# SSM kernel generation with 64-row TensorE tiles: phases and coarse decays as two products side by side

## The chip, the cores and the metric

The kernel runs on one core of a Trainium2 chip. A core has TensorE (matrix products, PE in the profile; its weight loads are PEld), VectorE (DVE), ScalarE (ACT), GpSimd (POOL) and SyncE (SP), which issues the DMA transfers; SBUF is its working memory and PSUM takes the products. Every engine works through its own instruction stream in order and waits on semaphores for the others. The metric is the device time of one execution in microseconds (us); lower is better.

## The reference, cut to what matters

Two branches are mixed by a gate. Branch A is a diagonal state-space layer: for each of D = 640 channels a kernel K of length L = 2048 is generated from N = 128 complex modes, and convolved with the input by FFT. Branch B is a feed-forward layer of width 1728 with a ReLU.

```
dt = exp(log_dt)
A = -exp(log_A_real) + 1j * A_imag
C = (C_real + 1j * C_imag) * dt[:, None]
P = exp((A * dt[:, None])[:, :, None] * pos[None, None, :])
K = 2.0 * einsum("dn,dnl->dl", C, P).real
...
y = irfft(rfft(u_t, 2L) * rfft(K, 2L), 2L)[:, :, :L]
a = y.T + u * D_skip
b = relu(x @ w1) @ w2
g = sigmoid((u * gate_w).sum(-1))
out = g * a + (1 - g) * b
```

## The kernel before

The work is added as tasks to a planner (class `Plan`). Each task has an engine, a queue, a booked duration, the tasks it depends on and the buffers it takes and frees. `run` (line 160) goes through the queues, picks the next task for each engine by priority and readiness, and emits its instructions; so the booked durations decide the order of the instructions on every engine, and the order is fixed when the kernel is built. On TensorE each task also has a mode, and a change of mode is booked at 0.2 us (line 108). All engine calls go through one helper, which is why all profile lines carry L228; operations are told apart by the names of their tiles.

The feed-forward branch (`feed_forward`, line 278) runs in 3 parts of 5, 5 and 4 blocks of 128 hidden units, each over 8 groups of 256 positions. Values are split in a high and a low float32r part (`xh`, `xl`, `w1h`, `w1l`, `hh`, `hl`, `w2h`, `w2l`), and three products stand for one float32 product. `hidden` (line 396) computes ReLU(x w1) with products of 256 columns, `sums` (line 442) the second layer with products of 320 columns; both write PSUM tiles `pf`. ScalarE takes the high part (`hh`), VectorE the low part (`hl`), and VectorE adds the sums into `q`. Weight tiles are split into `w1l` and `w2l` by VectorE. From the second part on, x is loaded again from DRAM (`xh`, `xl` from `xt`), and partial sums go out to `part` and come back as `q`.

The SSM kernel K is generated in 40 blocks of C = 16 channels (`ssm`, line 742). For each block c one tile R[c] of 128 rows (16 channels times 8 values: high and low parts of the angle per step, an offset angle, and the decay rate) by 128 modes is the stationary operand. It is multiplied with a constant table `tg` that has 128 rows and a block per channel:

- phases (line 792): `pg` = 16 channels x 64 positions, two products of 512 columns, table columns 0 to 1023;
- coarse decays (in `exponents`, line 815): `px` = 16 x 64, two products of 512 columns, table columns 1024 to 2047;
- fine decays (line 826): `pe` = 16 x 32, one product of 512 columns, table columns 2048 to 2559.

Row 8d + k of R belongs to channel d of the block, and the table is zero except where row and column belong to the same channel. So the first product of `pg` has entries only in rows 0 to 63, the second only in rows 64 to 127; the same holds for `px`.

The three are joined on TensorE to one visit (line 925). After a visit ScalarE rounds the phase (`cs`<-`pg`), VectorE takes the remainder (`sn`) and its absolute value (`cs`), ScalarE computes exponentials (`me`, `mg`) and sine and cosine, and VectorE multiplies them (`factors`, line 851: `G`, `mg`, `cs`, `sn`). Every second block `taps` (line 880) forms the kernel values in 128x32 tiles of TensorE (`pk`), VectorE turns them (`kt`), GpSimd adds the skip term and SP stores them to `kd`.

The convolution (`conv`, line 936) starts when all of `kd` is stored. It runs 5 rounds of 128 channels with small FFT matrices as 64x64 and 128x64 tiles of TensorE (`pc`): first stage for the kernel (`ck`) and the input (`ut`) with the table `tf`, second stage (`vk,tm` and `va,tm`), a product on VectorE (`t`), an inverse second stage (`t,tn`), turns on VectorE (`vk`, `va`) and an inverse first stage (`vk,tw`). Feed-forward products stand between its instructions where the planner found room.

Before all this, `params` (line 612) computes rates and angles from the inputs, and loads the table `t_g` in pieces of 512 columns, which ScalarE casts to float32r into `tg` (lines 719 to 728).

Of the kernel before, what the change touches and what calls it, by code (L numbers as in the profile page):

```python
# [10 lines left out]
F32 = mybir.dt.float32  # L11
F32R = mybir.dt.float32r
# [9 lines left out]
PARTS = (5, 5, 4)  # L22
CG = (0, 0, 0, 1, 2, 3, 4, 5)
FIRST = 7
BEHIND = 3

# [1 line left out]
def slots():  # L30
    return np.concatenate([np.arange(32, 64), np.arange(31, -1, -1)])
# [5 lines left out]
def tables():  # L37
    a = np.arange(64)
    k1 = 2 * np.arange(32)[None, :] + np.arange(2)[:, None]
    al = 2 * np.pi * (k1[..., None] + 0.25) * a / 64  # L40
    f1 = np.stack([np.cos(al), np.sin(al)]).transpose(3, 1, 0, 2).reshape(64, 128)
    w = np.stack([np.cos(al), np.sin(al)], axis=1) / 2048
    b = np.arange(32)
    om = 2 * np.pi * (k1[:, :, None, None] + 0.25 + 64 * b[None, None, :, None]) * b / 2048
    c, s = np.cos(om), np.sin(om)
    m = np.zeros((2, 2, 32, 32, 3, 32))
    n = np.zeros((2, 2, 32, 32, 2, 2, 32))
    iw = np.zeros_like(w)
    for p in range(2):
        ct, st = c[p].transpose(2, 0, 1), s[p].transpose(2, 0, 1)  # L50
        m[p, 0, :, :, 0], m[p, 0, :, :, 1] = ct, st
        m[p, 1, :, :, 0], m[p, 1, :, :, 1] = -st, ct
        m[p, :, :, :, 2] = m[p, :, :, :, 0]
        for g in range(32):
            h = p ^ (g & 1)
            ck, sk = c[p, g], s[p, g]
            re, im = np.stack([ck, -sk], axis=1), np.stack([sk, ck], axis=1)
            n[h, 0, :, g, 0], n[h, 1, :, g, 0] = re, -re
            n[h, 0, :, g, 1], n[h, 1, :, g, 1] = im, im
            iw[p, :, g // 2 * 2 + h] = w[p, :, g]  # L60

    pt, mg, me = np.zeros((16, 8, 16, 64)), np.zeros((16, 8, 16, 64)), np.zeros((16, 8, 16, 32))
    for d in range(16):
        pt[d, :2, d, :32], pt[d, :2, d, 32:], pt[d, 2:4, d, :32] = b, 32 * b + 16, 1
        mg[d, 4:6, d], me[d, 4:6, d] = 32 * slots(), b
    tg = np.concatenate([x.reshape(128, -1) for x in (pt, mg, me)], axis=1)
    f = lambda x: np.ascontiguousarray(x.astype(np.float32))
    return dict(t_g=f(tg), t_f1=f(np.tile(np.stack([f1, f1[slots()]], axis=1), (2, 1, 1))), t_w=f(iw.reshape(128, 64)),
                t_m=f(m.reshape(128, 32, 96)), t_n=f(n.reshape(128, 32, 128)))
# [180 lines left out]
class Kernel:  # L250
# [361 lines left out]
    def params(self):  # L612
        tc, nc, io, A = self.tc, self.nc, self.io, self.plan.add
# [65 lines left out]
        R = lambda f: (lambda V: f(V, *T_()))  # L679
# [36 lines left out]
        done = [*last['a'], *last['c'], *self.rows_st[0], *self.rows_st[1]]  # L716
        self.tg_done, tok = [], self.plan.token
        self.plan.ring('tgs', 2)
        for h in range(5):
            s_ = tok('tgs')  # L720

            def load(h=h):
                tl['tgs', h] = tl['pp'].tile([128, 512], F32, name="tgs", bufs=2)
                D_.dma_start(tl['tgs', h], io['t_g'][:, h * 512:h * 512 + 512])
            a = A('SP', 'tg', 0.62, load, [self.prm0], take=[s_], kb=256, rank=6)
            self.late_loads.append(a)
            self.tg_done.append(A('ACT', 'tg', 0.63, lambda h=h: S.copy(self.tg[:, h * 512:h * 512 + 512], tl['tgs', h]),
                                  [a], use=[s_], rank=4))

        p_ = tok('px')  # L730

        def cm_pe():
            px = self.psg.tile([128, 4, 256], F32, name="px")
            tl['pe'] = px.rearrange("p a b -> p (a b)")[:, :D].rearrange("p (t d) -> p t d", d=128)
            for t in range(NT):
                self.E.transpose(tl['pe'][:, t], tl['mx'][:, t], self.ident)
        a = A('PE', 'cm', 1.1, cm_pe, last['c'], take=[p_], rank=2, mode='f')
        self.cm_done = A('ACT', 'cm', 1.2, lambda: S.copy(self.cm[:].rearrange("p (t d) -> p t d", d=128), tl['pe']), [a],
                         use=[p_], rank=1)
        return [*done, *self.tg_done, self.cm_done, a]  # L740

    def ssm(self, C=16):
        tc, nc, io, A, tok, ring = self.tc, self.nc, self.io, self.plan.add, self.plan.token, self.plan.ring
# [5 lines left out]
        self.xp = gk  # L749
        self.c_ps, self.psg = self.cm_enter(name="psg", bufs=1, space=PSUM)  # L750
        self.cm = gk.tile([128, D], F32, name="cm")
        self.tg = gk.tile([128, 2560], F32R, name="tg")
        dsk = gk.tile([128, n // 2, 2 * Q], F32, name="dsk")
        nc.gpsimd.memset(dsk, 0.0)
        for k, v in dict(pg=1, px=1, pk=1, sc=5, mg=4, G=2, kt=2, PS=2).items():
# [10 lines left out]
        st = {}  # L766
# [4 lines left out]
        opened = self.prm_shut = A('PY', 'open', 0, go, self.params())  # L771
        self.prm_open = opened
        R, rows = {}, {}
# [14 lines left out]
        tasks, f = {}, {}  # L788
# [3 lines left out]
        def phases(c):  # L792
            p_, s_ = tok('pg'), tok('sc')
            rd, r_ = rows[c]

            def pe():
                p = self.psg.tile([128, 4, 256], F32, name="pg")
                pf = p.rearrange("p d j -> p (d j)")
                st['pg'] = pf.rearrange("p (d j) -> p d j", j=64)
                for h in range(2):  # L800
                    x = slice(h * 512, h * 512 + 512)
                    self.E.matmul(pf[:, x], R[c], self.tg[:, x], start=True, stop=True)

            def whole():
                st['sc', c] = [st['gp'].tile([128, C, 64], F32, name=k, bufs=5) for k in ("sn", "cs")]
                S.copy(I(st['sc', c][1]), st['pg'])
            a = visit[c, 1] = A('PE', None, 0.5, pe, [rd, opened, *self.tg_done], take=[p_], use=[r_], rank=2, mode='f')
            b = acts[c, 0] = A('ACT', None, 0.97, whole, [a], take=[s_], use=[p_], rank=2)
            d = A('DVE', 'g1', 1.14, lambda: V.tensor_sub(st['sc', c][0], st['pg'], I(st['sc', c][1])), [b],
                  use=[p_, s_], rank=1)  # L810
            e = A('DVE', 'g1', 0.62, lambda: V.tensor_scalar(I(st['sc', c][1]), I(st['sc', c][0]), 0x7fffffff, None,
                                                             op0=ALU.bitwise_and), [d], use=[s_], rank=1, port=True)
            tasks[c] = dict(s=s_, abs=e)

        def exponents(c):
            p_, m_ = tok('px'), tok('mg')
            rd, r_ = rows[c]

            def pe():
                p = self.psg.tile([128, 4, 256], F32, name="px")  # L820
                pf = p.rearrange("p d j -> p (d j)")
                st['px', c] = pf.rearrange("p (d j) -> p d j", j=64)
                for h in range(2):
                    x = slice(h * 512, h * 512 + 512)
                    self.E.matmul(pf[:, x], R[c], self.tg[:, 1024 + h * 512:1536 + h * 512], start=True, stop=True)
                q = st['pe', c] = self.psg.tile([128, C, 32], F32, name="pe")
                self.E.matmul(q.rearrange("p d j -> p (d j)"), R[c], self.tg[:, 2048:], start=True, stop=True)

            def exps(k):
                def go():  # L830
                    if k:
                        st['mg', c] = st['gp'].tile([128, C, 64], F32, name="mg", bufs=4)
                        S.activation(st['mg', c], st.pop(('px', c)), AF.Exp)
                    else:
                        st['me', c] = st['gp'].tile([128, C, 32], F32, name="me", bufs=4)
                        S.activation(st['me', c], st.pop(('pe', c)), AF.Exp)
                return go
            a = visit[c, 2] = A('PE', None, 0.7, pe, [rd, opened, *self.tg_done], take=[p_], use=[r_], rank=2, mode='f')
            b = acts[c, 1] = A('ACT', None, 0.52, exps(0), [a], take=[m_], use=[p_], rank=2, mode='exp')
            d = acts[c, 2] = A('ACT', None, 0.96, exps(1), [b], use=[p_, m_], rank=2, mode='exp')  # L840
            e = A('POOL', 'g2', 1.2, lambda: P.tensor_mul(st['me', c], st['me', c], self.cm[:, c * C:c * C + C, None]
                                                          .to_broadcast([128, C, 32])), [b, self.cm_done], use=[m_])
            s_ = tasks[c]['s']
            h, o = TWO_PI, tasks[c]['abs']
            x = acts[c, 3] = A('ACT', None, 1.0, lambda: S.activation(st['sc', c][0], st['sc', c][0], AF.Sin, scale=h), [o],
                  use=[s_], rank=2, mode='sin')
            y = acts[c, 4] = A('ACT', None, 1.06, lambda: S.activation(st['sc', c][1], st['sc', c][1], AF.Sin, scale=-h,
                                                          bias=self.half_pi), [o], use=[s_], rank=2, mode='sin')
            tasks[c].update(m=m_, exps=[d, e], trig=[x, y])
# [60 lines left out]
        visit, acts = {}, {}  # L910
        for c in range(n):
            if c % 8 == 0:
                load_rows(c)
            phases(c)
            exponents(c)
            factors(c)
# [10 lines left out]
        for p in range(n // 2 + 1):  # L927
            c = 2 * p
# [280 lines left out]
```

## Time and profile before

| | |
|---|---|
| time, median of 3 runs | 719.56 us (719.55 to 720.75) |
| profiled execution | 716.08 us, its span 714.3 us |
| granted TensorE clock, mean | 0.99 |
| visits of the generation on TensorE | 40, from 102.6 to 395 us |
| first product of the convolution | 441.6 us |
| first product of its second stage | 470.6 us |

The rows quoted below are of two kinds. A row of the order of time begins with the start and the length of an instruction or a run of equal ones in us; then come engine, line, operation, output<-inputs, and on TensorE the tile (rows*columns of the array that are used), the shape of the operand that streams and the count. Lengths on TensorE overlap, because products are pipelined and their ends are modelled; what one product costs is read from start to start. A row of busy times by stretch gives the stretch, its length, and for each engine the time that it was busy and the number of its instructions, then the granted clock, the share of the DMA engines' time and the rate.

### The profile page before, as it was taken

How to read it: one execution, taken by the hardware profiler on the slowest of the kernel's cores; microseconds unless marked ns; L12 is line 12 of the kernel's file. 1: busy time of each engine (PE TensorE's matmuls, PEld its weight loads, DVE VectorE, ACT ScalarE, POOL GpSimd, SP SyncE). 2: the span in 40 equal slices, each digit the busy share in tenths (PEclk: the TensorE clock that was granted, in tenths of full speed). 3: DMA queues.
4: the chain of work that ended last, by engine and by line, in shares of the span. 5: the costliest groups of instructions: out<-in, count | busy, mean ns of one | idle time of the engine just before them, and what ended most of it. 6: DMA issues, size and time to landing. Idle time of an engine off the chain costs nothing.

```text
span 714.3 us, 21601 instructions
## 1 busy us (share of the span) xinstructions
PE 672.8 (94%) x9469; PEld 594.5 (83%) x9469; DVE 574.4 (80%) x833; ACT 389.2 (54%) x572; POOL 71.4 (10%) x81
## 2 busy tenths in 40 slices
PE   5989999999999999999999999999699999699897
PEld 4989999889898899999999998887297587487695
DVE  4689628989999999999999873667969879479675
ACT  4353339989888978878888720134151341241330
POOL 1000002111122211122111100000000000010020
PEclk9999999999999999999999999999999999899999
DMA  8963764334556424423422659951643924731534
GB/s 202 260 236 137 272 207 148 86 124 164 164 206 225 146 93 140 160 68 132 160 93 91 235 198 315 290 180 50 140 109 119 225 76 161 139 88 56 121 97 96
DMA packets 92005, 110.83 MB, mean 155 GB/s; under 512 B 30912, under 2 KB 73416, under 8 KB 91656
## 3 DMA queue, kind: packets, MB, share of 16 engines
q1 hardware_dynamic: 91912, 109.46, 51.2%
q8 instruction: 74, 1.21, 0.7%
q14 instruction: 19, 0.16, 0.1%
HBM read 70.24 MB, written 39.20 MB: 153 GB/s over the span
## 4 chain that ended last, share of the span: by engine, by line
PE 69%; DVE 16%; ACT 8%; issue 2%; DMA 2%; SPq 2%; POOLq 0%; DVEq 0%; ACTq 0%
PE pf L228 42%; PE pc L228 18%; PE pk L228 5%; DVE sn L228 3%; ACT cs L228 2%; DVE vk L228 2%; PE pg L228 2%; DVE G L228 2%; DVE mg L228 2%; SPq L228 2%; PE px L228 1%; DVE cs L228 1%; DVE hl L228 1%; ACT L228 1%; ACT sn L228 1%
## 5 line engine op out<-in xcount | busy, mean ns | idle before, releaser
L228 PE MATMUL pf<-xh,w1h 128*128 128x256 f32 x560 | 163.3, 292 | 0.3 <-DVE hl L228 0.3
L228 PE MATMUL pf<-xl,w1h 128*128 128x256 f32 x560 | 160.4, 287 | 0.4 <-DVE xl L228 0.4
L228 PE MATMUL pf<-xh,w1l 128*128 128x256 f32 x560 | 159.9, 285 | 0.0
L228 PE MATMUL pf<-w2h,hh 128*128 128x320 f32 x448 | 140.4, 316 | 3.9 <-DVE hl L228 3.2
L228 PE MATMUL pf<-w2l,hh 128*128 128x320 f32 x448 | 137.9, 311 | 0.0
L228 PE MATMUL pf<-w2h,hl 128*128 128x320 f32 x448 | 126.8, 312 | 0.8 <-DVE hl L228 0.8
L228 PEld LDWEIGHTS pf<-xh,w1h 128*128 128x128 f32 x560 | 109.1, 195 | 6.7 <-issue 4.2
L228 PEld LDWEIGHTS pf<-xl,w1h 128*128 128x128 f32 x560 | 109.2, 195 | 1.6 <-DVE xl L228 0.7
L228 PEld LDWEIGHTS pf<-xh,w1l 128*128 128x128 f32 x560 | 109.3, 195 | 0.0
L228 ACT ACTIVATE hh<-pf 128x512 fp32r<-128x512 f32 (+1 forms) x64 | 34.8, 543 | 127.7 <-PE pf L228 122.0
L228 PEld LDWEIGHTS pf<-w2h,hh 128*128 128x128 f32 x448 | 84.1, 188 | 16.3 <-issue 7.2
L228 PEld LDWEIGHTS pf<-w2l,hh 128*128 128x128 f32 x448 | 84.2, 188 | 5.5 <-issue 4.9
L228 DVE TENSOR_TENSOR t<-pc,kw 128x512 f32<-128x512 f32 x80 | 53.8, 691 | 42.0 <-ACT kw L228 42.0
L228 PEld LDWEIGHTS pf<-w2h,hl 128*128 128x128 f32 x448 | 80.7, 188 | 8.3 <-issue 5.9
L228 POOL TENSOR_TENSOR me<-me,cm 128x512 f32<-128x512 f32 x40 | 50.5, 1262 | 182.3 <-DVE cs L228 103.9
L228 DVE TENSOR_TENSOR mg<-mg,cs 128x1024 f32<-128x1024 f32 x40 | 58.2, 1454 | 1.1
L228 DVE SCALAR_TENSOR_TENSOR hl<-pf,hh 128x512 fp32r<-128x512 f32 (+1 forms) x64 | 39.7, 623 | 20.4 <-ACT hh L228 20.2
L228 ACT COPY kw<-pc 128x256 f32<-128x256 f32 x80 | 29.7, 373 | 47.5 <-PE pc L228 44.9
L228 ACT ACT_TABLE_LOAD x42 | 53.9, 1283 | 0.8
L228 DVE TENSOR_TENSOR sn<-pg,cs 128x1024 f32<-128x1024 f32 x40 | 48.7, 1218 | 6.5 <-ACT cs L228 6.0
L228 PE MATMUL pc<-va,tm 64*64 64x128 f32 x1280 | 53.4, 275 | 0.0
L228 ACT CAST cs<-pg 128x1024 int32<-128x1024 f32 x40 | 40.4, 1010 | 22.0 <-PE pg L228 21.8
(138 smaller groups left out, 1221.5 us busy)
## 6 DMA issues: line engine op xcount, KB each, us to landing
part<-q SPq DMA_DIRECT2D x16, 640.0 KB, 3.8
xh<-xt SPq DMA_DIRECT2D x16, 640.0 KB, 6.6
xl<-xt SPq DMA_DIRECT2D x16, 640.0 KB, 5.2
q<-part SPq DMA_DIRECT2D x16, 640.0 KB, 4.1
ws<-in_B_w_dram SPq DMA_DIRECT2D x22, 320.0 KB, 3.5
xs<-in_A_u_dram SPq DMA_DIRECT2D x16, 320.0 KB, 4.0
xt<-xh SPq DMA_DIRECT2D x8, 640.0 KB
xt<-xl SPq DMA_DIRECT2D x8, 640.0 KB
```

Of the source, the lines that this page charges most:

```text
L228: return lambda *a, **k: self._tc.keep_in_program_order(f(*a, **k))
```

## The change

The table keeps one 8-channel block of 64 rows for phases and one for coarse decays, each 512 columns wide, and holds it twice, in rows 0 to 63 and 64 to 127. The fine decays keep their table. The whole table has 1536 columns instead of 2560, and is loaded and cast in three pieces instead of five. Each of the two products of `pg` and `px` takes 64 rows of R[c] and the same 64 rows of the table, and writes the half of the output that it wrote before, in its own PSUM bank. The product for `pe` is unchanged, with 128 rows. The planner's booked durations for the visit go from 0.5 + 0.7 to 0.3 + 0.55 us; the tasks' mode stays 'f', as for feed-forward products. An unused constant goes.

```diff
-    tg = np.concatenate([x.reshape(128, -1) for x in (pt, mg, me)], axis=1)
+    tg = np.concatenate([np.tile(x[:8, :, :8].reshape(64, -1), (2, 1)) for x in (pt, mg)] + [me.reshape(128, -1)], axis=1)
...
-        for h in range(5):
+        for h in range(3):
             s_ = tok('tgs')
...
-        self.tg = gk.tile([128, 2560], F32R, name="tg")
+        self.tg = gk.tile([128, 1536], F32R, name="tg")
...
                 for h in range(2):
-                    x = slice(h * 512, h * 512 + 512)
-                    self.E.matmul(pf[:, x], R[c], self.tg[:, x], start=True, stop=True)
+                    r = slice(64 * h, 64 * h + 64)
+                    self.E.matmul(pf[:, h * 512:h * 512 + 512], R[c][r], self.tg[r, :512], start=True, stop=True)
...
-            a = visit[c, 1] = A('PE', None, 0.5, pe, [rd, opened, *self.tg_done], take=[p_], use=[r_], rank=2, mode='f')
+            a = visit[c, 1] = A('PE', None, 0.3, pe, [rd, opened, *self.tg_done], take=[p_], use=[r_], rank=2, mode='f')
...
+                q = st['pe', c] = self.psg.tile([128, C, 32], F32, name="pe")
                 for h in range(2):
-                    x = slice(h * 512, h * 512 + 512)
-                    self.E.matmul(pf[:, x], R[c], self.tg[:, 1024 + h * 512:1536 + h * 512], start=True, stop=True)
-                q = st['pe', c] = self.psg.tile([128, C, 32], F32, name="pe")
-                self.E.matmul(q.rearrange("p d j -> p (d j)"), R[c], self.tg[:, 2048:], start=True, stop=True)
+                    r = slice(64 * h, 64 * h + 64)
+                    self.E.matmul(pf[:, h * 512:h * 512 + 512], R[c][r], self.tg[r, 512:1024], start=True, stop=True)
+                self.E.matmul(q.rearrange("p d j -> p (d j)"), R[c], self.tg[:, 1024:], start=True, stop=True)
...
-            a = visit[c, 2] = A('PE', None, 0.7, pe, [rd, opened, *self.tg_done], take=[p_], use=[r_], rank=2, mode='f')
+            a = visit[c, 2] = A('PE', None, 0.55, pe, [rd, opened, *self.tg_done], take=[p_], use=[r_], rank=2, mode='f')
```

More of the change, by code (lines that the diff above doesn't have):

```diff
@@ L24 @@
 FIRST = 7
-BEHIND = 3
 def slots():
```

## The prediction

> **What bounds the kernel now.** I read the page first, then the busy times by stretch. The stretches are cut where the program changes: the first visit of the SSM generation (102.7 us), the last one (395), the first product of the convolution (441.7), its second stage (470.6).
>
> ```profile
> span 714.3 us, 21601 instructions
> ...
> PE 672.8 (94%) x9469; PEld 594.5 (83%) x9469; DVE 574.4 (80%) x833; ACT 389.2 (54%) x572; POOL 71.4 (10%) x81
> ```
>
> ```profile
> core 0: us, PE busy (x) PEld busy (x) DVE busy (x) ACT busy (x) POOL busy (x), PEclk, DMA share, GB/s
> ...
> 102.70:395.00 292.30, 284.14 (x3988) 266.04 (x3987) 273.74 (x378) 253.22 (x299) 57.53 (x57) 1.00 0.41 135
> 395.00:441.70 46.70, 45.89 (x570) 44.49 (x572) 30.92 (x46) 18.99 (x26) 1.78 (x3) 1.00 0.79 242
> 441.70:470.60 28.90, 28.75 (x215) 21.83 (x215) 19.45 (x25) 2.63 (x4) 0.00 (x0) 1.00 0.92 287
> 470.60:520.00 49.40, 43.57 (x886) 31.79 (x889) 38.08 (x51) 18.23 (x43) 0.00 (x0) 1.00 0.47 119
> ```
>
> TensorE is busy 94% of the span, but the reader is to see three kinds of stretch. From 102.7 to 395, TensorE idles 292.3 - 284.1 = 8.2 us and VectorE 18.6 us: both are nearly full and wait on each other. From 395 to 470.6 TensorE alone is full (1.0 us idle in 75.6) and VectorE has a third free. From 470.6 to 520 TensorE has holes of 5.8 us; the chain of waits of that stretch says why:
>
> ```profile
> by line: PE pc L228 45.0%; DVE vk L228 31.4%; DVE va L228 10.6%; issue 3.0%; DVE hl L228 2.2%; PE pf L228 2.1%; DVE t L228 1.4%; ACT yj L228 1.3%; ACT yo L228 1.3%; DVE yj L228 1.3%; ACT kw L228 0.8%
> ```
>
> There the convolution's own chain runs, over VectorE's turns for 42%; feed-forward products (pf) hold 2.1% of it and only fill holes.
>
> **One visit.** Phases (pg), coarse decays (px) and fine decays (pe) of one block stand together on TensorE, 40 times:
>
> ```profile
> 203.01 0.31 PE L228 MATMUL pf<-w2l,hh 128*128 128x320 f32 x1
> 203.16 0.63 PE L228 MATMUL pg<-tg,PS 128*128 128x512 f32 x2
> 203.62 0.64 PE L228 MATMUL px<-tg,PS 128*128 128x512 f32 x2
> 204.09 0.40 PE L228 MATMUL pe<-tg,PS 128*128 128x512 f32 x1
> 204.33 0.30 PE L228 MATMUL pf<-w2h,hl 128*128 128x320 f32 x1
> ```
>
> Start to start, a visit takes 204.33 - 203.16 = 1.17 us: five products of 0.234 us. Starts are used because the durations overlap. A feed-forward product of 320 columns takes 203.16 - 203.01 = 0.15 us (0.147 over a run of them), one of 256 columns 0.12 us (below).
>
> **What the edit does to a visit.** The two products of pg become two of 64 rows each, on the upper and lower half of the array; so do those of px. If the halves run side by side, two of five streams go: -0.47 us. But the array's shape changes twice per visit, 128 rows to 64 and back for pe. The trace has no 64x128 tile, so the price is taken from its nearest rows, the 64x64 tiles of the convolution between feed-forward products:
>
> ```profile
> 493.97 0.28 PE L228 MATMUL pf<-xl,w1h 128*128 128x256 f32 x1
> 494.09 0.28 PE L228 MATMUL pf<-xh,w1l 128*128 128x256 f32 x1
> 494.30 1.09 PE L228 MATMUL pc<-ut,tf 64*64 64x512 f32 x8
> 495.31 0.39 PE L228 MATMUL pf<-xh,w1h 128*128 128x256 f32 x1
> 495.54 0.28 PE L228 MATMUL pf<-xl,w1h 128*128 128x256 f32 x1
> ```
>
> ```profile
> 489.76 1.90 PE L228 MATMUL pc<-ck,tf 64*64 64x512 f32 x16
> 491.59 0.39 PE L228 MATMUL pf<-xh,w1h 128*128 128x256 f32 x1
> ```
>
> Going in, the gap is 0.21 instead of 0.12 us: +0.09. Sixteen products take 1.83 us and eight take 1.01, so eight cost 0.82 by themselves and 0.19 comes once, for weights that could not be loaded ahead and for emptying the array. Coming out, the first pf holds 0.23 instead of 0.12: +0.11. Together 0.39 us per round trip. A visit then takes 3 x 0.234 + 0.39 = 1.09 us and saves 0.08, in all 40 x 0.08 = 3.2 us, a sixth of the 18.7 that two streams a visit would give. The bounds: no price for the change of shape, 0.70 us a visit and 18.7 us saved; halves one after the other, 1.17 + 0.39 = 1.56 us and 15.6 us lost. I take 1.09, since switches and tiles side by side are both in the rows.
>
> The Trainium skill (TensorEngine Tiling (Array Packing), Tiling Modes, Key Properties) says that a change of the tiling mode, not of the tile alone, drains TensorE. That row tiles of full width pay this too no run here shows; by the page they do, and the sum stays at 3.2 us instead of going towards 18.7.
>
> That halves run side by side, the rows show for another type:
>
> ```profile
> 511.74 1.08 PE L228 MATMUL pc<-vk,tw 128*64 128x512 f32 x4 [0.72 <-DVE va L228]
> ```
>
> Four products of 128 rows take as long there as eight of 64 rows (1.09 us at 494.30), both over 512 columns.
>
> **What the edit does to the order.** The kernel's planner now books a visit at 0.85 us instead of 1.2, and puts more feed-forward work ahead of each. In the two programs' listed orders I counted pf products (256 and 320 columns, at 0.12 and 0.147 us). Before the first visit both have 345 and 240. Before the last visit: 1146 and 900 in the old order, 1200 and 950 in the new: +13.9 us. Before the first product of the convolution +9.9 us; before its second stage (1395 and 1104 against 1437 and 1104) +5.0 us. By the end of its first round both have 1440 and 1128, and from there the TensorE orders agree. So the change acts on the first 520 us.
>
> VectorE does more before the last visit too: two splits hl, one of half size, three sums q, three weight splits w1l. Their prices, start to start:
>
> ```profile
> 402.61 0.69 DVE L228 SCALAR_TENSOR_TENSOR hl<-pf,hh 128x512 fp32r<-128x512 f32 x1
> 403.22 0.68 DVE L228 TENSOR_TENSOR G<-mg,sn 128x512 f32<-128x512 f32 x1
> ...
> 405.39 0.82 DVE L228 TENSOR_TENSOR w1l<-ws,w1h 128x640 fp32r<-128x640 f32 x1
> 406.13 0.48 DVE L228 TENSOR_TENSOR q<-pf,q 128x320 f32<-128x320 f32 x1
> 406.53 0.68 DVE L228 TENSOR_TENSOR cs<-me,cs 128x512 f32<-128x512 f32 x1
> ```
>
> 0.61, 0.74 and 0.40 us: 1.2 + 0.3 + 1.2 + 2.2 = +4.9 us.
>
> **The sum.** At the last visit TensorE has 13.9 - 3.1 = 10.8 us more to do, VectorE 4.9. If TensorE's 8.2 us of waiting stay, the visit comes 10.8 us later; if they vanish, since the others are now ahead of it, 2.6 us later. I take the middle, +6.7: TensorE falls behind VectorE by 5.9 us, which can't empty all the waits. From there to the second stage 51.0 us of pf stand instead of 59.9, in the stretch that TensorE fills alone: -8.9. In the first round two splits hl leave VectorE's chain:
>
> ```profile
> 493.98 0.69 DVE L228 SCALAR_TENSOR_TENSOR hl<-pf,hh 128x512 fp32r<-128x512 f32 x1
> 494.56 4.64 DVE L228 STREAM_TRANSPOSE vk<-va 128x512 f32<-128x512 f32 x4
> ```
>
> 2 x 0.58 = -1.2 us; the 5.0 us of pf missing there lay in TensorE's holes and give nothing. Sum: 6.7 - 8.9 - 1.2 = -3.4 us, between -7.5 and +0.7.
>
> The smaller table (three loads and casts instead of five) counts as nothing:
>
> ```profile
> L228 PE MATMUL pg<-tg,PS x80: 387/397/502, 102.6 to 395.1; 128*128 128x512 f32 x80
> ...
> L228 ACT CAST tg<-tgs x5: 612/622/634, 38.5 to 62.3; 128x512 fp32r<-128x512 f32 x5
> ```
>
> The casts end 40 us before the first visit, which stands behind the same pf work in both orders; ScalarE would gain 2 x 0.62 us if that cover were gone. The SP order changes at the hand-over:
>
> ```profile
> 431.90 0.54 SPq L228 DMA_DIRECT2D ut<-in_A_u_dram  x1
> ...
> 438.13 0.33 SPq L228 DMA_DIRECT2D xh<-xt  x1
> ...
> 442.76 2.80 SPq L228 DMA_DIRECT2D ck<-kd  x4
> ```
>
> Now xh and xl (1.28 MB) go ahead of ut and the tables, and ck goes behind two stores of part. At the 287 GB/s of the stretch ut lands 4.5 us later against the last kd. It used to be issued 9.8 us ahead of the convolution's first product, which hides it barely.
>
> Profile against profile that is 716.08 - 3.4 (span 714.3 plus 1.8 outside it). The median of the runs shown stands 3.5 us above the profiled execution; the difference is carried to it: 719.56 - 3.4 = 716.2 us.
>
> **Rivals.** (1) The change of shape costs little for tiles of full width. Then a visit takes 0.70 to 0.85 us and saves 0.32 to 0.47, the planner's booking holds, and the last visit comes about when it did: 0 - 8.9 - 1.2 = -10 us, 709.5. VectorE's 4.9 us keep it from more. For it: no row shows 64x128. Against it: the 64x64 rows.
>
> (2) It ends slower. The halves, each a single-pass product that brings a column per step into two PSUM banks, share a path and run one after the other. At 1.56 us a visit the last visit comes 13.9 + 15.2 - 8.2 = 21 us later, 21 - 8.9 - 1.2 = +11 us, 730.5. In between, each 0.1 us of a visit is worth 4 us, so the gain is gone at about 1.18 us a visit. For it: no single-pass half is in the trace, and the tiled rows pass half as many columns in the time. Against it: tiles side by side in f32.
>
> (3) Transfers at the hand-over set the pace. From 395 to 470.6 they move 46.7 x 242 + 28.9 x 287 = 19.6 MB; less some 1.3 MB that the earlier pf work takes along, 18.3 MB have to pass in 66.7 us. At the mean of the stretch (259 GB/s) that takes 70.7 us: 4 us of the gain go, 720. For it: a DMA share of 0.92. Against it: TensorE hardly waits there.
>
> **How the numbers follow.** Forecast 45%, rival 1 20%, rival 2 17%, rival 3 18%. About 0.2% (1.4 us) is what a measurement of this kernel can tell from no change. The forecast's own range, -7.5 to +0.7 (712 to 720.3), lies for three quarters under 718.1; with rival 1 and a little of rival 3 that makes faster 0.56. Same: part of the forecast and half of rival 3, 0.15. Slower: rival 2, the rest of rival 3 and a tail of the forecast, 0.29. The range is 708 to 727: from rival 1 with a little beyond, up to two thirds of the way to rival 2.
>
> **What would show it.** In the changed profile: visits, start to start, of 1.09 us (0.7 to 0.85 for rival 1, 1.5 for rival 2), pg's two products starting within some 10 ns of each other; the last visit at some 402 us, the convolution's second stage near 468; TensorE idle under 8 us up to the last visit; no wait of pc for ck or ut. The forecast is wrong if visits leave 1.0 to 1.18 us, or if pc waits for a DMA for more than 2 us.

## The result and the profile after

The change takes 722.83 us (median of 20 runs, 719.95 to 727.11), the kernel before 717.57 us on the same chip (median of 20 runs, 714.72 to 720.75): a ratio of 1.0078 with a 95% interval of 1.0063 to 1.0094. It is slower by 0.8%, where 716.2 us and a small gain were forecast. The profiled execution took 721.99 us; of before 716.08. The page of the change, first its span and busy times:

```profile
span 720.1 us, 21599 instructions
...
PE 669.4 (93%) x9469; PEld 577.6 (80%) x9469; DVE 575.7 (80%) x833; ACT 388.1 (54%) x570; POOL 72.8 (10%) x81
```

TensorE is busy 3.4 us less than before and the span is 5.8 us longer. The work was saved; waits of 9 us came in. The last visit, in order of time (start, length, engine, line, operation, tile, operand, count), first its pg of before, then the change:

```profile
394.85 0.63 PE L228 MATMUL pg<-tg,PS 128*128 128x512 f32 x2
```

```profile
405.37 0.31 PE L228 MATMUL pf<-w2l,hh 128*128 128x320 f32 x1
405.61 0.50 PE L228 MATMUL pg<-tg,PS 64*128 64x512 f32 x2
405.95 0.40 PE L228 MATMUL px<-tg,PS 64*128 64x512 f32 x2
406.27 0.50 PE L228 MATMUL pe<-tg,PS 128*128 128x512 f32 x1
406.61 0.30 PE L228 MATMUL pf<-w2h,hl 128*128 128x320 f32 x1
```

The gap into the visit is 405.61 - 405.37 = 0.24 us where pf alone has 0.15, so +0.09; from there to the next pf are 1.00 us. The visit costs 1.09 us, as forecast (the median of 39 visits in this trace has the same 1.00 us behind the gap), and the two halves of a pair, start to start, take 0.34 and 0.32 us where two full products took 0.46 and 0.47. The halves run side by side. Where the time went instead, the busy times by stretch show, cut at the same events as before (first visit, last visit, first product of the convolution, second stage):

```profile
103.20:405.60 302.40, 292.53 (x4091) 263.40 (x4090) 280.73 (x387) 258.24 (x307) 58.96 (x57) 1.00 0.44 143
405.60:450.40 44.80, 42.97 (x539) 40.66 (x538) 27.38 (x41) 16.14 (x21) 1.77 (x3) 1.00 0.65 186
450.40:474.10 23.70, 23.68 (x178) 17.16 (x178) 17.96 (x22) 1.20 (x2) 0.00 (x0) 1.00 1.05 301
```

Up to the last visit 302.4 us in place of 292.3, and TensorE's idle time is 9.9 us, not less than the 8.2 of before. From there to the second stage 68.5 us in place of 75.7. The same events as groups (duration, then first and last start, tile and operand):

```profile
L228 PE MATMUL pg<-tg,PS x80: 465/494/505, 103.2 to 405.6; 64*128 64x512 f32 x80
...
L228 PE MATMUL pc<-vk,tm x640: 268/269/473, 474.1 to 689.2; 64*64 64x128 f32 x160
...
L228 PE MATMUL pc<-ck,tf x160: 589/589/1110, 450.4 to 658.1; 64*64 64x512 f32 x160
...
L228 PE MATMUL pc<-vk,tw x80: 592/593/643, 515.3 to 708.3; 128*64 128x512 f32 x80
```

Against before the last visit (405.6, before 394.85) is 10.8 us late, the first product of the convolution (450.4, before 441.6) 8.8, the second stage (474.1, before 470.6) 3.5, and the inverse first stage of round 1 (515.3, before 511.7) 3.6. The remaining 2.2 us come in the later rounds. Each side is one profile here: that of before lies 1.5 us under the median of its 20 runs, that of the change 0.8 us under its own, so a shift of 1 or 2 us may be chance.

### The profile page after: what moved, and what is told of

It reads as the page before. It is cut to its first block, busy times and chain, and to the rows that moved or that the text cites. A ratio compares the mean times of both kernels' runs of the same rounds, so it can differ in the third digit from the quotient of the medians.

```text
span 720.1 us, 21599 instructions
## 1 busy us (share of the span) xinstructions
PE 669.4 (93%) x9469; PEld 577.6 (80%) x9469; DVE 575.7 (80%) x833; ACT 388.1 (54%) x570; POOL 72.8 (10%) x81
## 4 chain that ended last, share of the span: by engine, by line
PE 71%; DVE 13%; ACT 8%; issue 4%; DMA 3%; SPq 1%; POOLq 0%; DVEq 0%; ACTq 0%
PE pf L228 44%; PE pc L228 19%; PE pk L228 4%; ACT cs L228 3%; DVE sn L228 2%; PE pg L228 2%; DVE mg L228 1%; SPq L228 1%; PE pe L228 1%; DVE G L228 1%; DVE hl L228 1%; DVE cs L228 1%; ACT L228 1%; DVE va L228 1%; DMA tf<-in_t_f_dram 1%
## 5 line engine op out<-in xcount | busy, mean ns | idle before, releaser
L228 POOL TENSOR_TENSOR me<-me,cm 128x512 f32<-128x512 f32 x40 | 52.4, 1309 | 170.0 <-DVE cs L228 104.4
L228 ACT COPY kw<-pc 128x256 f32<-128x256 f32 x80 | 29.7, 373 | 41.1 <-PE pc L228 38.3
```

Source lines behind the costliest of these rows:

```text
L228: return lambda *a, **k: self._tc.keep_in_program_order(f(*a, **k))
```

## The experiments

All ratios are to the kernel before, over several rounds on one chip. The shifts in us come from one profile each; a shift is the start of the same event against the profile that is named. Where an expectation speaks of the order theory, it is this: the time follows from how much pf the planner's order puts ahead of each point, and not from what a visit costs.

**Products and order apart.** The change has two parts, the tiles and the booked durations. Each was run without the other. First the tiles with the old booking, whose TensorE order is that of before:

```diff
-            a = visit[c, 1] = A('PE', None, 0.3, pe, ...
+            a = visit[c, 1] = A('PE', None, 0.5, pe, ...
-            a = visit[c, 2] = A('PE', None, 0.55, pe, ...
+            a = visit[c, 2] = A('PE', None, 0.7, pe, ...
```

> The 64-row products with the old booked durations (0.5 and 0.7), so TensorE's order is that of before. Order theory (the loss comes from the order that the booking of 0.85 us makes, the products themselves save 0.08 us a visit): 0 to 3.2 us faster than before, ratio 0.9955 to 1.000. Tile theory (the 64-row products and the changes of the array's shape cost more than the visits show): as slow as the change, ratio 1.005 or more. Scatter theory (any shift of the order costs some us at random): no forecast, 0.995 to 1.01.

Measured: 716.28 us against 718.06, ratio 0.997 (0.9955 to 0.9986). Then the old full products with the change's booking (0.5 and 0.7 to 0.3 and 0.55 in the kernel before, nothing else):

> The old products of 128 rows with the new booked durations (0.3 and 0.55), so TensorE's order is that of the change, at 1.17 us a visit. Order theory: slower than the change, by up to 3.2 us: 5 to 9 us above before, ratio 1.007 to 1.012. Tile theory: about as fast as before, ratio under 1.003. The last visit by the order theory 10.8 to 14 us later than before.

Measured: 725.99 us, ratio 1.0117 (1.0098 to 1.0136), with the last visit 14.4 us later than before. Two bookings between, 0.42 + 0.67 = 1.09 us, which is what a tiled visit takes, with the tiles and with the full products:

> The 64-row products, booked at what a visit takes (0.42 and 0.67, in sum 1.09 us). Feed-forward work ahead of the last visit is 4.4 us more than before, ahead of the convolution's first product the same. Order theory: 1 to 4 us faster than before, ratio 0.994 to 0.999. Tile theory: 1.005 or more.

> The old products of 128 rows with the bookings 0.42 and 0.67: the order of e3 with visits of 1.17 us. Order theory: 0 to 3.2 us slower than e3, within 2 us of before (ratio 0.997 to 1.003). Tile theory: faster than e3 by the 5 us that it puts on the tiles.

Measured: 720.91 us, ratio 1.005 (1.0033 to 1.0067), and 723.58 us, ratio 1.0078 (1.0054 to 1.0101). The six cells, the change's from its own comparison; the pf is counted in the listed orders as in the prediction, at 0.12 and 0.1467 us a product:

| booking of a visit | full products | 64-row tiles | pf ahead of the last visit / of the second stage, us |
|---|---|---|---|
| 1.20 us | 718.06 (before) | 716.28 | 269.5 / 329.4 |
| 1.09 us | 723.58 | 720.91 | 273.9 / 329.4 |
| 0.85 us | 725.99 | 722.83 (the change) | 283.4 / 334.4 |

Down a column the order costs 5.5 and 7.9 us with full products, and 4.6 and 6.5 with tiles. Along a row the tiles save 1.8, 2.7 and 3.2 us. The intervals of the ratios make each of these differences uncertain by some 2 us; the tiled run is the faster one in all three rows. So the tiles gain, in the size that was forecast for them (3.2), and the booking of the change loses twice that. But the pf ahead is not the whole of it: with 1.09 as much of it stands ahead of the second stage as with 1.20, and the time is 4.6 to 5.5 us worse. The expectations of the order theory for 1.09 were both missed (0.994 to 0.999 for the tiles, 0.997 to 1.003 for the full products).

**Where the orders lose.** From the first visit to the second stage, one row for each of four kernels: before, tiles with 1.20, full products with 1.09, the change.

```profile
102.60:470.60 368.00, 358.87 (x4768) 332.46 (x4766) 324.21 (x448) 274.84 (x329) 59.31 (x60) 1.00 0.50 160
```

```profile
102.40:468.10 365.70, 354.74 (x4769) 316.56 (x4768) 323.83 (x448) 274.56 (x329) 59.48 (x60) 1.00 0.51 161
```

```profile
101.90:474.70 372.80, 360.84 (x4769) 334.00 (x4767) 324.32 (x448) 274.53 (x329) 59.48 (x60) 1.00 0.50 158
```

```profile
103.20:474.10 370.90, 359.18 (x4807) 321.22 (x4806) 326.07 (x449) 275.57 (x330) 60.73 (x60) 1.00 0.51 159
```

Before has 4768 TensorE products there and 9.1 us of idle time (368.00 - 358.87). The tiles take 4.1 us off the busy time; 1.8 us of that come back as waits, so 2.3 remain. The change has 42 feed-forward products more than the tiles with 1.20, the 5.0 us of pf (the row shows 38 more, since some records of other products are missing), and is 5.2 us longer, most of it busy time (+4.4). With 1.09 and full products the work is that of before, yet the stretch is 4.8 us longer: 2.8 us of waiting, and 2.0 us in which the same products take longer. The granted clock (the third number from the end) falls there, for 3.4 us. Full products with 1.09, about a wait of pk for `cs`:

```profile
424.35 0.25 PE L228 MATMUL pk<-mg,cs 128*32 128x64 f32 x2 [1.54 <-DVE cs L228]
```

```profile
422.70:426.10 3.40, 1.57 (x93) 1.30 (x93) 2.94 (x5) 0.59 (x1) 0.00 (x0) 1.00 0.87 301
426.10:429.50 3.40, 3.40 (x58) 3.23 (x48) 0.72 (x1) 0.41 (x1) 0.21 (x1) 0.50 0.74 292
```

Tiles with 1.09, about a visit that waits for `sn`:

```profile
356.17 0.50 PE L228 MATMUL pg<-tg,PS 64*128 64x512 f32 x2 [2.06 <-DVE sn L228]
```

```profile
353.40:356.80 3.40, 1.34 (x9) 0.75 (x8) 3.40 (x5) 3.37 (x4) 1.04 (x1) 1.00 0.50 165
356.80:360.20 3.40, 3.40 (x14) 3.27 (x13) 2.68 (x6) 3.40 (x4) 0.00 (x0) 0.50 0.03 7
```

TensorE idles 1.83 of 3.4 us with the full products, in a wait of 1.54 us and smaller ones, and 2.06 us with the tiles, in one single wait, while VectorE is busy for most of the time; then the clock is 0.50 for 3.4 us. The kernel before shows how much idle time it takes. First pieces of at most 0.9 us in its round 1, then waits of at most 1.27 us in a later round:

```profile
502.00:505.40 3.40, 1.85 (x17) 0.42 (x16) 3.40 (x6) 0.00 (x0) 0.00 (x0) 1.00 0.14 58
505.40:508.80 3.40, 2.02 (x21) 0.47 (x16) 3.40 (x5) 0.00 (x0) 0.00 (x0) 1.00 0.55 156
```

```profile
614.60:618.00 3.40, 0.89 (x24) 0.64 (x24) 1.38 (x2) 0.74 (x2) 0.00 (x0) 1.00 0.24 68
618.00:621.40 3.40, 2.38 (x40) 1.99 (x44) 1.30 (x3) 1.78 (x7) 0.00 (x0) 0.51 0.44 108
```

Idle for 1.55 of 3.4 us, TensorE keeps its clock; idle for 2.51, it loses half of it, though no wait was longer than 1.27 us. In all 14 traces the recorded clock changes on a grid of 3.41 us. From 70 us to shortly before the end, every step of this grid at full clock with 53% or more of idle time was followed by half the clock (27 of 27), none with less than 47% was (0 of 2552), and half of the 12 between were. These shares go by the recorded ends, which are modelled. Up to the second stage the waits of the two tiled kernels, first with 1.20, then with 1.09 (what waits, for what, us in all, times, the longest):

```profile
PE pf L228 <- DVE hl L228: 5.1, 7, 1.3
PE pg L228 <- DVE sn L228: 2.7, 4, 1.3
```

```profile
PE pg L228 <- DVE sn L228: 4.9, 6, 2.1
PE pf L228 <- DVE hl L228: 2.1, 5, 0.6
PE pk L228 <- DVE cs L228: 1.5, 1, 1.5
```

With 1.09 the waits gather at pg, which needs VectorE to have taken the last block's phases (`sn`) out of PSUM, and single waits are longer. So two things make an order dear: pf that it takes out of the convolution and puts ahead of it, and waits that it makes, the more so where they halve the clock. In the 1.09 orders the waits themselves are the larger part: 3.4 us at half the clock are 1.7 us of the 4.8. Waits and clock fit the loss in the one profile of each; why this order makes these waits is not shown.

**What 5 us of work cost in each place.** In the tiled kernel with 1.20, 5.0 us of pf were issued a second time in one of three places, all other order kept: the first product of an accumulation group up to nine times more, of which the last counts.

```diff
-                        self.E.matmul(st['sb', g, j], ..., start=k == 0, stop=k == 3 * n - 1)
+                        for z in range(again(0.147) if k == 0 else 1, 0, -1):
+                            self.E.matmul(st['sb', g, j], ..., start=k == 0, stop=z > 1 or k == 3 * n - 1)
```

> The 64-row tiles with the visits booked at 1.20 us, and 5.0 us of pf products issued a second time between visits 37 and 39 (the first product of four accumulation groups, up to nine times more each; the last of each is the one that counts). The order of everything else stays. Theory that TensorE sets the pace there: last visit 5 us later than with 1.20 (397.4 in place of 392.4 us), second stage 5 us later (473 in place of 468.1), end 4 to 6 us later, so 720.5 to 722.5 us (ratio to before 1.003 to 1.007). Theory that slack of VectorE, the transfers or the exchange of buffers takes it up: second stage less than 2 us later, 716 to 718.5 (0.997 to 1.001).

> The same 5.0 us of repeated pf products, between the last visit and the first convolution product. Theory that TensorE sets the pace in the hand-over too: first convolution product 5 us later than with 1.20 (444 in place of 439.1 us), 720.5 to 722.5 us (1.003 to 1.007). Theory that the hand-over has a pace of its own (transfers of tables, VectorE): product 0 to 2.5 us later, 716 to 719 (0.997 to 1.002).

> The same 5.0 us of repeated pf products, behind the first product of the second stage (vk,tm), between the products of the first convolution round. Theory that TensorE has holes there which pf fills for nothing: product 720 and the end 0 to 2 us later than with 1.20 (490.5 us), 716 to 718.5 us (0.997 to 1.001). Theory that TensorE sets the pace there too, so that work has the same price in each place and the order alone cannot cost: 5 us later, 720.5 to 722.5 (1.003 to 1.007).

Measured: 719.67 us, 1.0043 (1.0025 to 1.0061); 721.7 us, 1.0067 (1.0048 to 1.0086); 718.7 us, 1.002 (1.0003 to 1.0037), where the kernel without the addition has 0.997. The first two fit TensorE's pace (the first with 719.67 us just under its range); the third lies between its two theories. The ratios are 0.007, 0.010 and 0.005 above that, each uncertain by some 0.002; the kernel without the addition ran on another chip than these three. Groups of the kernel without the addition and of the three, in that order (with one line more in the file, the helper is L229):

```profile
L228 PE MATMUL pg<-tg,PS x80: 467/494/505, 102.4 to 392.4; 64*128 64x512 f32 x80
...
L228 PE MATMUL pc<-vk,tm x640: 266/269/418, 468.1 to 683.4; 64*64 64x128 f32 x160
...
L228 PE MATMUL pc<-vk,tw x80: 592/592/644, 511.1 to 701.8; 128*64 128x512 f32 x80
```

```profile
L229 PE MATMUL pg<-tg,PS x80: 465/495/507, 102.0 to 395.9; 64*128 64x512 f32 x80
```

```profile
L229 PE MATMUL pg<-tg,PS x80: 468/494/506, 104.7 to 394.7; 64*128 64x512 f32 x80
...
L229 PE MATMUL pc<-vk,tm x640: 267/269/418, 474.3 to 690.8; 64*64 64x128 f32 x160
```

```profile
L229 PE MATMUL pc<-vk,tm x640: 266/269/418, 468.3 to 687.8; 64*64 64x128 f32 x160
...
L229 PE MATMUL pc<-vk,tw x80: 592/593/644, 512.9 to 706.0; 128*64 128x512 f32 x80
```

Between the first and the last visit stand 293.9 us instead of 290.0: +3.9. From the last visit to the second stage 79.6 instead of 75.7: +3.9. In round 1, from the second stage to its end, 44.6 instead of 43.0: +1.6. The first two prices are firm: where the work is the same, the other profiles of this order have 290.0 and 75.6 us again. The third is not: in seven profiles with the same feed-forward work in round 1 it takes 41.1 to 43.0 us, so the price there may be 1.6 or 3.5 by these alone, and the kernel with 1.50 below takes 41.3 us with 33 products more in it. So the same work costs 3.9 us before the convolution's second stage and less, perhaps nothing, behind it. The totals stand in the same order, though only the second and the third are clear of each other, and they are 1 to 3 us above these shifts: from the inverse first stage on, these profiles take up to 3 us longer with the same order of TensorE. That part is not explained.

Why round 1 takes work cheaply, its end shows in before and in the change (from some 21 us behind the start of the second stage to the inverse first stage):

```profile
492.00:511.70 19.70, 15.22 (x110) 9.14 (x109) 19.70 (x22) 1.20 (x2) 0.00 (x0) 1.00 0.37 120
```

```profile
495.00:515.30 20.30, 12.84 (x86) 5.00 (x77) 19.50 (x21) 0.37 (x1) 0.00 (x0) 0.83 0.18 53
```

VectorE (the third busy time) is full there in both, and the stretch takes 20 us whether TensorE has 110 products in it or 86. Without the others TensorE stands still:

```profile
500.49 0.31 PE L228 MATMUL pf<-w2h,hl 128*128 128x320 f32 x1
506.06 3.72 PE L228 MATMUL pc<-ck,tf 64*64 64x512 f32 x16 [5.26 <-issue]
```

The sixteen products behind the 5.26 us take 3.72 us, at half the clock, where before they took 1.90. The Trainium skill (TensorE: Matmul & The Clock Gate, What's actually happening) has the clock fall to half behind an idle window of some 3.4 us. The 5.26 us agree with that. The falls above do not, if an idle window is one without any work: there no wait is longer than 2.1 us, about half of 3.4 us in all is enough, and the measurement decides.

**The table tf at the hand-over.** In the change's chain of waits the first product of the convolution waits for a transfer that is asked for last:

```profile
437.93 5.35 SPq L228
443.28 0.04 issue
443.32 7.05 DMA tf<-in_t_f_dram
450.38 0.04 issue
450.42 2.81 PE pc L228 x24
```

```diff
-            return A('SP', 'tab', 0.62, go, [opened], kb=..., rank=3)
+            return A('SP', 'tab', 0.62, go, [opened], kb=..., rank=rank)
...
-        tf = table('tf', [128, 2, 128], 't_f1')
+        tf = table('tf', [128, 2, 128], 't_f1', 1)
```

> The change with one edit: the table tf of the first convolution products is asked for ahead of the ut transfers, so that it no longer lands last (in the profile of the change the request for tf stood at 443.3 us behind 6 us of requests, and the first product waited 7 us for it). The planner also puts 4.6 us less pf ahead of the first product, and the same pf ahead of the second stage, within 0.7 us. Theory that the transfer of tf set the first product in the change: the product starts 2 to 5 us earlier than 450.4 us, and what it gains stays to the end, so 718 to 720.5 us (ratio to before 1.000 to 1.004). Theory that the time goes by the pf ahead of the second stage (vk,tm) and by what is left for the convolution's holes: second stage still at 473 to 475 us, total 722 to 723.5 (1.006 to 1.008).

Measured: 723.95 us, ratio 1.0089 (1.007 to 1.0109).

```profile
L228 PE MATMUL pc<-vk,tm x640: 266/269/469, 474.1 to 688.9; 64*64 64x128 f32 x160
...
L228 PE MATMUL pc<-ck,tf x160: 588/589/1110, 445.1 to 658.0; 64*64 64x512 f32 x160
```

The first product comes 5.3 us earlier and the second stage at 474.1 us as without. The total lies a little above the range of the second theory and far from the first. TensorE was nearly full while tf was late (busy 12.07 of the 12.50 us before 450.4, with 0.4 us of waiting for tf): pf stood in for pc, and the same pf is due ahead of the second stage in either case. The transfer was late and cost next to nothing.

**Longer bookings.** If an early visit is good, a booking above 1.20 us might be better still. Three tiled kernels, with 0.55 + 0.75, 0.65 + 0.85 and 0.70 + 0.90 us:

> The 64-row tiles with the planner's two visits booked at 0.55 + 0.75 = 1.30 us in place of 0.30 + 0.55. pf ahead of the last visit as before (269.5 us), ahead of the first convolution product 309.5 against 304 with 1.20, ahead of the second stage 329.4 against 324.8. Theory that the time follows the pf ahead of each point: last visit within 1 us of the run with 1.20 (392.4 us), second stage 3 to 5 us later (471 to 473 us), total 717 to 719 (ratio 0.999 to 1.002). Theory that a later visit in the planner's timetable gives earlier real ones and the rest is taken up by holes: 714 to 716.5 (0.994 to 0.997).

> The 64-row tiles with the visits booked at 0.65 + 0.85 = 1.50 us. pf ahead of the last visit 260.0 us (269.5 with 1.20), of the first convolution product 296.3 (304), of the second stage 316.6 (324.8): some 8 to 9 us of pf go behind the second stage, where conv round 1 has PE holes of 5 to 9 us. Theory that the time follows the pf ahead of each point and that these holes take it up: last visit 383 to 387 us, second stage 460 to 463 us, end 3 to 6 us earlier than with 1.20, so 710 to 714 (ratio 0.989 to 0.994). Theory that VectorE or the transfers pace the visits from there on, or that the holes are full already: last visit 388 to 392, and the pf moved is paid in the convolution in full, 716 to 720 (0.997 to 1.003).

> The 64-row tiles with the visits booked at 0.70 + 0.90 = 1.60 us. pf ahead of the last visit 255.3 us, of the first convolution product 291.7, of the second stage 296.3: 28 us less than with 1.20 before the second stage, all of it left for the rounds of the convolution. Theory that the time follows the pf ahead and the holes take it up: second stage 440 to 450 us, of the 28 us at most some 9 find holes in round 1 and the rest is paid there, 708 to 714 (0.986 to 0.994). Theory that the holes are full: last visit earlier, but the total 717 to 724 (0.998 to 1.008), with PE idle in 440 to 540 us below 4 us.

The figures 304 and 324.8 that the first two give for 1.20 are not that order's; it has 309.5 and 329.4, as 1.30 has. The pf theory then says no shift for 1.30, and 12.8 us less work ahead of the second stage for 1.50. Measured: 717.0 us, 0.9998 (0.9977 to 1.0018); 725.84 us, 1.0112 (1.0092 to 1.0132); 746.8 us, 1.0409 (1.0376 to 1.0442). The first lies at the lower end of the total that the pf theory gave with the wrong figures; its last visit came at 395.1 us and its second stage at 470.1, 2.7 and 2.0 us later than with 1.20. The other two lie outside both of their theories. The last visit with 1.50 came at 399.2 us, not at 383 to 387, with 1.60 at 405.5, and its second stage at 470.5, not at 440 to 450. The stretch of the visits with 1.50 and its waits:

```profile
102.90:399.20 296.30, 277.66 (x3918) 247.90 (x3917) 271.78 (x372) 252.65 (x298) 54.50 (x57) 0.97 0.40 129
```

```profile
PE pg L228 <- DVE sn L228: 9.2, 6, 2.3
PE pg L228 <- issue: 4.5, 2, 2.2
```

With less pf between the visits TensorE comes to pg before VectorE has freed it, idles 18.6 us, and loses clock (0.97). Booked shorter than 1.20 us, visits get more pf ahead of them; booked at 1.50, less than fills the time that VectorE takes. Of the six bookings 1.20 has the lowest time; the interval of 1.30 overlaps with its own. No rule of the pf ahead told the times of 1.09, 1.30, 1.50 and 1.60, so the scatter theory of the first expectation, some us for any shift of the order, is not ruled out for them.

**Both together.** The tiles with 1.20 and tf asked for first, which in this order moves 4.6 us of pf behind the start of the second stage and leaves the generation as it is:

> The 64-row tiles booked at 1.20 us, with the table tf asked for ahead of the ut transfers; the planner then puts 5.4 us less pf ahead of the first convolution product and 4.6 us less ahead of the second stage (324.8 in place of 329.4 us), the last visit unmoved. Theory that TensorE's work ahead of each point sets the time and the round takes up what moved: second stage at 463 to 466 us in place of 468.1, 711 to 715 us (0.990 to 0.996), the fastest so far. Theory that another work is late by then (the kd and ut transfers, VectorE): second stage still at 468, 716 to 718 (0.997 to 1.000).

Measured: 712.56 us against 717.29, ratio 0.9937 (0.9914 to 0.9961), faster than before and than the change.

```profile
L228 PE MATMUL pg<-tg,PS x80: 470/494/506, 103.0 to 393.0; 64*128 64x512 f32 x80
...
L228 PE MATMUL pc<-vk,tm x640: 267/269/418, 463.2 to 680.9; 64*64 64x128 f32 x160
...
L228 PE MATMUL pc<-vk,tw x80: 592/593/645, 507.7 to 699.4; 128*64 128x512 f32 x80
```

From the last visit to the second stage stand 70.2 us (75.7 without), and round 1 takes 44.5 (43.0): 5.5 us gained for 4.6 us of pf and 1.5 given back. Second stage and total are those of the first theory, though the gain is more than the price of 3.9 for 5.0 us says. That the pf that moved pays, and not the earlier table, is supported by the same edit in the change's order, which moved 0.7 us of pf and gained nothing. Its interval touches that of the tiles with 1.20 alone (0.9955 to 0.9986), and the two were not compared in one batch.

## Why the prediction was wrong

**The visit was right.** 1.09 us by its own rows, pairs side by side, a price for the change of shape as that of the 64x64 tiles. The rivals that rested on it, cheap changes of shape and halves one after the other, are out. The saving of 3.2 us agrees with the 1.8 to 3.2 us in the three rows of the table. The rule of the Trainium skill that was weighed there (TensorEngine Tiling (Array Packing), Key Properties: a change of the mode drains) agrees with the 0.09 us on the way in.

**The failed step is the middle of +6.7 us at the last visit**: "TensorE falls behind VectorE by 5.9 us, which can't empty all the waits". The last visit came 10.8 us late, the upper end; the waits did not shrink at all. Idle time from the first to the last visit is 8.2 us before and 9.9 with the tiles and 1.20; the order with 0.85 leaves it there, at 8.4 us with full products and 9.9 with the tiles, though it puts 13.9 us of pf in. The waits on record are each for one tile (`sn`, `hl`, `xl`, `kt` and a few more). That work put elsewhere does not fill such a wait is the reading that fits; it was not tested by itself. In the experiment 5.0 us of work just before a visit took 0.7 us out of the idle time and cost 3.9. That 10.8 is met to the tenth is luck: TensorE's busy time grew by 8.4 us and not by 10.8, its idle time by 1.7, and the first visit came 0.6 later. Of the 9.2 us between the forecast for the span (-3.4) and the measured +5.8, this step makes 4.1.

**The term -8.9 us from the last visit to the second stage** measured 68.5 - 75.7 = -7.2: the pf left, but TensorE's idle time in the stretch rose from 1.0 to 1.85 us, of which 1.0 is one wait of pf for `w2l`, which VectorE splits. The statement that the 5.0 us of pf missing in round 1 "lay in TensorE's holes and give nothing" fits: round 1 takes 41.2 us against 41.1. An order that takes 5.0 us out of there pays for them elsewhere, +4.4 us of busy time against the tiles with 1.20; it is not the only loss, since the orders with 1.09 lose 4.6 to 5.5 us and take nothing out. Round 1 was to give 1.2 us for two splits less and gave none, with a hole that halves the clock in their place.

**Not in the sum at all** were 2.2 us in the rounds behind, where the TensorE orders hardly differ. The runs with repeated work show such rests of up to 3 us as well, and their cause stays open; the spread of single runs is as large.

So the sum by measured terms is +10.8 - 7.2 + 0.1 + 2.2 = +5.9 us, against the span's +5.8. **Rival 3**, the transfers, had its place right (the chain of waits goes over a table, with a DMA share of 1.05) and its price wrong: TensorE waited 0.4 us for it, and the order that asks for it earlier gains nothing. The bound "-7.5 to +0.7" was too narrow above: it took the upper end of the waits, +10.8, but not the losses behind it.

## What to carry to other kernels

Where a planner orders the work by booked durations, the booking is part of the change: run new products with the old order and old products with the new order, since the two effects can have different signs, as here (some -2 to -3 and +5 to +8 us). An engine's idle time in a stretch is no reservoir that more work empties; ask for each wait what it waits for, and price work by the place where it lands: here 5 us cost 3.9 where TensorE sets the pace and less where VectorE does. The booking that is true to the hardware need not be the best: 1.09 us was measured and 1.20 was faster.

## What the hardware showed

- Pairs of products of 64 rows by 128 columns over 512 columns run side by side in float32r, and a pair with its weights takes 0.32 to 0.34 us where two full products take 0.46.
- What halved the granted clock was not the length of one wait but the share of idle time: 1.55 of 3.4 us in short pieces left it full, 2.51 us in pieces of at most 1.27 us halved it, and so did 1.83 and 2.06 us about a single wait. In the 14 traces the border lies between 47% and 53% of a step of 3.41 us, counted on a fixed grid, and the clock then stays at half for at least one such step.
